# Chunk 1 transposed by TensorE instead of by DMA, rows of chunk 2 in one burst behind chunk 1's, casts of chunk 2's last batch sooner, rows of chunk 3 behind its transpose

## The chip, the cores and the metric

One core of one Trainium2 chip. The metric is the device time of one execution in microseconds. The granted clock is the share of full speed that the throttle allowed TensorE, 1.00 being all of it. Positions inside an execution are microseconds from the start of the profiled span, which is some 1.7 us shorter than the time.

## The reference

A retention recurrence (4 batches, 8 heads, 768 steps, head size 64), then a two-layer MLP with a tanh GELU (512 to 2048 to 512), all in float32:

```python
for t in range(S):
    state = gamma * state + einsum('bhd,bhe->bhde', k[:, :, t], v[:, :, t])
    y[:, :, t] = einsum('bhd,bhde->bhe', q[:, :, t], state) / sqrt(D)
x = y.transpose(0, 2, 1, 3).reshape(B * S, H * D)
h = x @ w_in
g = 0.5 * h * (1 + tanh(c * (h + 0.044715 * h**3)))
out = g @ w_out
```

## The kernel before

The sequence is cut into six chunks of 128 steps. For each chunk and each of four batches the kernel loads the rows of q, k and v (256 KB each, on SyncE's queue), casts q and k to 16 bits on ScalarE, transposes them, forms the scores A, masks them on VectorE, forms y, updates the state, and then runs the expert layers over all four batches. Chunk c's output matmuls and expert matmuls carry chunk c+1's attention between them: `run` issues the units of one in order, and `after` says what comes behind each unit (a unit is a small group of matmuls, mostly eight, and the copies that follow). In the traces each engine works its own list in order, and so does SyncE: a DMA transpose that waits for its cast holds back every load behind it. In the kernel before, SyncE issued nothing from 63.37 to 65.35, when chunk 2's first two casts had just ended (65.32), and the v rows behind that transpose went out from 66.63 on.

Chunk 0 is transposed by TensorE, all later chunks by DMA:

```python
def mm_T(c, b):                       # used by chunk 0
    ps = bank("att", F16, (128, 2, NHP, 128), "qkT_ps")
    for i, nm in enumerate("qk"):
        for hp in range(NHP):
            nc.tensor.transpose(out=ps[:, i, hp], in_=pair(h16[nm, c, b], hp), identity=iden)
    pss["T", c, b] = ps
def ev_T(c, b, eng=nc.vector):
    copy_on(eng, qkT_tile(c, b), pss.pop(("T", c, b)))
def dma_T(c, b):                      # chunks 1 to 5
    nc.sync.dma_start_transpose(out=qkT_tile(c, b)..., in_=qk16.pop((c, b))...)
def prep_qk(c, b):
    prep1(AC, "q", c, b)              # cast on ScalarE
    prep1(AC, "k", c, b)
    dma_T(c, b)
# ... output units of chunk 0, with chunk 1's attention behind them
    3: [(preps, 1, 0), (loads, 1, "v1", "q2", "k2")],
    5: [(preps, 1, 1), (load_dec,), (loads, 1, "q3", "k3", "v2")],
    8: [(att_1A, 0), (preps, 1, 2), (loads, 1, "v3")],
    10: [(att_1A, 1)],
# ... expert units of chunk 1
    10: [(prep_qk, 2, 2)],
    11: [(g_sums, PO, 1, 0, 4, 1, 2), (loads, 3, "q0", "k0", "q1", "k1")],
# ... output units of chunk 1
    0: [(prep_qk, 2, 3), (loads, 3, "v0", "v1", "q2", "k2", "q3", "k3", "v2", "v3")],
    4: [(att_AY, 2, (0, 1), "h", 2, (2, 3), AC)],
```

`s_p`, `s_u` and `s_q` are ScalarE's copies of partial products out of PSUM. `s_g` are sums of g, made by GpSimd for chunk 1, that the output matmuls read.

## Time and profile before

| | before |
|---|---|
| median | 217.24 us (3 runs, 217.07 to 219.27) |
| span of the profiled run | 216.2 us |
| TensorE busy | 198.3 us, 92% |
| SyncE's DMA queue, packet time as a share of 16 engines' span | 51.9% |
| TensorE waits for DMA transposes | 7.4 us in two waits |

### The profile page before, as it was taken

How to read it: one execution, taken by the hardware profiler on the slowest of the kernel's cores; microseconds unless marked ns; L12 is line 12 of the kernel's file. 1: busy time of each engine (PE TensorE's matmuls, PEld its weight loads, DVE VectorE, ACT ScalarE, POOL GpSimd, SP SyncE). 2: the span in 40 equal slices, each digit the busy share in tenths (PEclk: the TensorE clock that was granted, in tenths of full speed). 3: DMA queues.
4: the chain of work that ended last, by engine and by line, in shares of the span. 5: the costliest groups of instructions: out<-in, count | busy, mean ns of one | idle time of the engine just before them, and what ended most of it. 6: DMA issues, size and time to landing. Idle time of an engine off the chain costs nothing.

```text
span 216.2 us, 4616 instructions
## 1 busy us (share of the span) xinstructions
PE 198.3 (92%) x1916; PEld 135.0 (62%) x1916; DVE 89.2 (41%) x195; ACT 101.4 (47%) x180; POOL 111.5 (52%) x112
## 2 busy tenths in 40 slices
PE   5789999839999957999999999999999999999993
PEld 1447648626777845864478854488844688644882
DVE  3445489227750415730128710418600456134421
ACT  2384564432459601646662447563266412367321
POOL 0595000112378998145999528999339991200000
PEclk9999999997999996999999999999999999999999
DMA  7999999999998999999995699943440000310004
GB/s 162 288 251 207 206 207 218 238 196 243 299 253 184 176 227 232 229 225 249 233 232 100 27 271 273 235 104 69 97 194 3 2 3 2 133 64 0 0 15 182
DMA packets 102837, 35.28 MB, mean 163 GB/s; under 512 B 96544, under 2 KB 101024, under 8 KB 102816
## 3 DMA queue, kind: packets, MB, share of 16 engines
q1 hardware_dynamic: 90624, 23.45, 51.9%
q0 software_dynamic: 5664, 9.44, 17.9%
q10 hardware_dynamic: 6528, 2.10, 3.8%
q8 instruction: 15, 0.25, 0.5%
q14 instruction: 6, 0.05, 0.1%
HBM read 27.63 MB, written 6.29 MB: 157 GB/s over the span
## 4 chain that ended last, share of the span: by engine, by line
PE 69%; DMA 16%; ACT 5%; SPq 4%; POOL 3%; issue 1%; DVE 0%
PE h_ps L351 30%; PE o_ps L459 27%; DMA w_out<-in_moe_w_out_dram 7%; DMA k<-in_k_dram 5%; DMA qkT<-qk 4%; SPq L85 4%; PE y_ps L247 3%; PE a_ps L210 3%; PE y_ps L234 3%; PE o_ps L563 2%; ACT qk L145 2%; ACT g L367 2%; POOL qk L161 1%; PE s_ps L271 1%; POOL w_in L332 1%; POOL w_out L341 1%
## 5 line engine op out<-in xcount | busy, mean ns | idle before, releaser
L351 PE MATMUL h_ps<-xT,w_in 128*128 128x512 f16 (+2 forms) x488 | 87.5, 334 | 1.4 <-ACT g L367 1.1
L367 ACT ACTIVATE g<-h_ps 128x512 f16<-128x512 f32 (+1 forms) x98 | 57.2, 588 | 33.7 <-PE h_ps L351 33.7
L351 PEld LDWEIGHTS <-w_in 128*128 128x128 f16 x488 | 45.4, 98 | 38.7 <-issue 3.7
L223 DVE TENSOR_TENSOR a_sb<-a_ps,mask 128x512 f16<-128x512 f32 x48 | 30.1, 683 | 53.9 <-PE a_ps L210 53.9
L390 POOL TENSOR_TENSOR s_g<-g 128x512 f16<-128x512 f16 x32 | 36.9, 1153 | 13.2 <-ACT g L367 13.2
L459 PEld LDWEIGHTS <-s_g 128*128 128x128 f16 x320 | 30.5, 99 | 4.8 <-issue 0.2
L161 POOL TENSOR_TENSOR v<-v,cst 128x512 f16<-128x512 f32 x20 | 20.4, 1043 | 22.4 <-DMA v<-in_v_dram 17.7
L459 PE MATMUL o_ps<-t_w,s_g 128*128 128x256 f16 x240 | 28.5, 277 | 0.0
L459 PEld LDWEIGHTS <-g 128*128 128x128 f16 x240 | 23.5, 98 | 3.6
L390 POOL TENSOR_TENSOR s_g<-s_g,g 128x512 f16<-128x512 f16 x16 | 18.4, 1152 | 1.3
L390 POOL TENSOR_TENSOR s_g<-g,s_g 128x512 f16<-128x512 f16 x16 | 18.5, 1154 | 0.0
L459 PE MATMUL o_ps<-w_out,g 128*128 128x256 f16 x160 | 18.3, 273 | 0.0
L263 DVE TENSOR_TENSOR xT<-y_ps,dec 128x512 f16<-128x512 f32 x20 | 13.1, 687 | 11.9 <-PE y_ps L247 11.9
L210 PE MATMUL a_ps<-qkT 64*128 64x128 f16 x192 | 8.7, 225 | 7.7 <-DMA qkT<-qk 7.4
L492 POOL DMA_DIRECT2D out_dram<-o_sb x8 | 5.9, 737 | 18.0 <-DVE o_sb L390 14.4
L145 ACT CAST qk<-q 128x512 f16<-128x512 f32 x20 | 12.4, 618 | 5.4 <-DMA q<-in_q_dram 5.4
L482 ACT COPY s_u<-o_ps 128x512 f32<-128x512 f32 (+1 forms) x6 | 3.1, 516 | 22.8 <-PE o_ps L459 17.5
L145 ACT CAST qk<-k 128x512 f16<-128x512 f32 x20 | 12.4, 619 | 2.7 <-DMA k<-in_k_dram 2.7
L210 PEld LDWEIGHTS <-qkT 64*128 64x128 f16 x192 | 5.6, 97 | 12.2 <-DMA qkT<-qk 7.8
L488 ACT COPY o_sb<-o_ps 128x512 f32<-128x512 f32 (+1 forms) x5 | 2.7, 544 | 22.4 <-PE o_ps L459 22.4
L390 DVE TENSOR_TENSOR s_g<-g 128x512 f16<-128x512 f16 x16 | 6.7, 421 | 12.6 <-ACT g L367 12.6
L390 DVE TENSOR_TENSOR o_sb<-o_ps,s_p 128x512 f32<-128x512 f32 (+1 forms) x7 | 4.3, 615 | 17.5 <-ACT qk L145 8.0
(59 smaller groups left out, 167.9 us busy)
## 6 DMA issues: line engine op xcount, KB each, us to landing
k<-in_k_dram SPq DMA_DIRECT2D x22, 256.0 KB, 4.3
q<-in_q_dram SPq DMA_DIRECT2D x22, 256.0 KB, 4.3
v<-in_v_dram SPq DMA_DIRECT2D x22, 256.0 KB, 4.2
out_dram<-o_sb POOLq DMA_DIRECT2D x10, 512.0 KB, 3.7
w_in<-in_moe_w_in_dram POOLq DMA_DIRECT2D x4, 512.0 KB, 8.8
w_out<-in_moe_w_out_dram POOLq DMA_DIRECT2D x4, 512.0 KB, 14.1
q<-in_q_dram ACTq DMA_DIRECT2D x2, 256.0 KB, 3.9
v<-in_v_dram ACTq DMA_DIRECT2D x2, 256.0 KB, 5.3
```

The lines of the kernel that those rows point to most:

```text
L85: eng.dma_start(out=ld_tile(nm, c, b), in_=srcs[nm][b, :, c * C:(c + 1) * C, :].rearrange("h p d -> p h d"),)
L145: eng.copy(out=out, in_=in_)
L161: eng.tensor_tensor(out=t, in0=src, in1=cst[:, col:col + H].unsqueeze(2).broadcast_to([128, H, Dh]), op=ALU.mult,)
L210: nc.tensor.matmul(out=ps[j][:, hp], lhsT=t[j * 64:(j + 1) * 64, 1, hp], rhs=t[j * 64:(j + 1) * 64, 0, hp], start=True, stop=True,)
L223: nc.vector.tensor_tensor(out=s, in0=ps[j], in1=mask[:, j], op=ALU.mult)
L234: nc.tensor.matmul(out=y_ps[sl, hp], lhsT=st[sl, b, hp], rhs=qkT[c, b][sl, 0, hp], start=(hp == 0), stop=False, skip_group_check=True,)
L247: nc.tensor.matmul(out=y_ps[j * 64:(j + 1) * 64, hp], lhsT=h16["v", c, b][:, 2 * hp + j], rhs=a_sb[c, b, j][:, hp], start=(c == 0), stop=True,
L263: nc.vector.tensor_tensor(out=x, in0=ps, in1=dec, op=ALU.mult)
L351: nc.tensor.matmul(out=out, lhsT=w_in_sb[wi][:, kc, wr * 128:(wr + 1) * 128], rhs=xT[c][:, kc, t0:t1], start=(kc == 0), stop=(kc == NHP - ...
L367: nc.scalar.activation(out=out, in_=in_, func=AF.Gelu_apprx_tanh, scale=1.0)
L390: eng.tensor_tensor(out=out, in0=in0, in1=in1, op=op)
L459: nc.tensor.matmul(out=po, lhsT=lhs(c, lk, fp, a), rhs=rhs(rk, fp), start=(new and fp == 0 and (last or a == 0)), stop=(stop and fp == NP ...
```

## The change

Its intent is to take TensorE's two waits for DMA transposes away. (1) Chunk 1, whose rows and transposes all crowd into the queue at once, goes through TensorE. (2) The rows of chunk 2 are issued right behind chunk 1's. (3) Batch 3 of chunk 2 is cast four units sooner (behind expert unit 12 of 0 to 15, instead of behind the first output unit), and chunk 3's rows are queued behind its transpose instead of partly ahead.

```diff
     def prep_qk(c, b):
         prep1(AC, "q", c, b)
         prep1(AC, "k", c, b)
-        dma_T(c, b)
+        if c > 1:
+            dma_T(c, b)
+    def att_T(b, eng=VE):
+        mm_T(1, b)
+        ev_T(1, b, eng)
-    loads(1, "q0", "k0", "q1", "k1", "v0")
+    loads(1, "q0", "k0", "q1", "k1", "v0", "q2", "k2", "v1", "q3", "k3")
+    load_dec()
+    loads(1, "v2", "v3")
+    for nm in ("qk", "v"):
+        loads(2, *[x + str(b) for b in range(B) for x in nm])
 # output units of chunk 0
-            3: [(preps, 1, 0), (loads, 1, "v1", "q2", "k2")],
-            5: [(preps, 1, 1), (load_dec,), (loads, 1, "q3", "k3", "v2")],
-            8: [(att_1A, 0), (preps, 1, 2), (loads, 1, "v3")],
+            3: [(preps, 1, 0)],
+            5: [(att_T, 0), (preps, 1, 1)],
+            7: [(att_1A, 0)],
+            8: [(att_T, 1)],
+            9: [(preps, 1, 2)],
             10: [(att_1A, 1)],
-            11: [(mm_Y, 0, "h"), (ev_Y, 1, 0), (preps, 1, 3), (loads, 2, "q0", "k0", "q1", "k1")],
-            12: [(mm_Y, 1, "att"), (ev_Y, 1, 1), (mm_s, 1, (0,))],
+            11: [(mm_Y, 0, "h"), (att_T, 2, AC), (ev_Y, 1, 0)],
+            12: [(mm_Y, 1, "att"), (ev_Y, 1, 1), (mm_s, 1, (0,)), (preps, 1, 3)],
 # expert units of chunk 1 (the other loads of chunk 2 leave their places here too)
+            0: [(att_T, 3)],
-            11: [(g_sums, PO, 1, 0, 4, 1, 2), (loads, 3, "q0", "k0", "q1", "k1")],
+            11: [(g_sums, PO, 1, 0, 4, 1, 2)],
+            12: [(prep_qk, 2, 3), (load, 3)],
 # output units of chunk 1
-            0: [(prep_qk, 2, 3), (loads, 3, "v0", "v1", "q2", "k2", "q3", "k3", "v2", "v3")],
```

More of the change, by code (lines that the diff above doesn't have):

```diff
@@ L747 @@
     )
-    loads(2, "q2", "k2", "q3", "k3")
     run(
@@ L761 @@
             5: [(mm_Y, 3, "o"), (ev_Y, 1, 3)],
-            6: [(att_S, 1, 3), (prep_qk, 2, 0), (loads, 2, "v0", "v1")],
+            6: [(att_S, 1, 3), (prep_qk, 2, 0)],
             7: [(g_sums, PO, 1, 4, 8, 0, 1)],
-            8: [(prep_qk, 2, 1), (loads, 2, "v2", "v3")],
+            8: [(prep_qk, 2, 1)],
             10: [(prep_qk, 2, 2)],
-            11: [(g_sums, PO, 1, 0, 4, 1, 2), (loads, 3, "q0", "k0", "q1", "k1")],
+            11: [(g_sums, PO, 1, 0, 4, 1, 2)],
+            12: [(prep_qk, 2, 3), (load, 3)],
             14: [(att_AY, 1, (), "o", 2, (0, 1), None), (prep1, PO, "v", 2, 0), (prep1, PO, "v", 2, 1)],
```

## The prediction

> **What bounds the kernel now.** I read the page's slices first, then TensorE's waits from 30 us on, then TensorE's timeline around each wait, then windows over the same stretches, and last the queues that feed the waits. TensorE is busy for 92% of the span, so what can be gained is where it isn't. The page's two TensorE rows:
>
> ```profile
> PE   5789999839999957999999999999999999999993
> PEclk9999999997999996999999999999999999999999
> ```
>
> Each digit is 5.4 us. Apart from the start and the tail there are two holes, at slices 9 and 16, and the granted clock falls in the slice of each hole or the one after. The waits of TensorE from 30 to 100 us (total us, times, longest) name what made them:
>
> ```profile
> PE a_ps L210 <- DMA qkT<-qk: 7.4, 2, 3.9
> PE o_ps L563 <- ACT s_p L541: 0.9, 1, 0.9
> ```
>
> So two waits for DMA transposes of q and k cost 7.4 us, and one wait for a ScalarE copy 0.9. TensorE's timeline (start, duration, what, idle before) shows both waits and what follows them:
>
> ```profile
> 43.06 1.04 PE L563 MATMUL o_ps<-t_w,s_g 128*128 128x256 f16 x8
> 47.61 0.40 PE L210 MATMUL a_ps<-qkT 64*128 64x128 f16 x8 [3.52 <-DMA qkT<-qk]
> 47.94 1.74 PE L563 MATMUL o_ps<-t_w,s_g 128*128 128x256 f16 x8
> ...
> 82.54 0.61 PE L210 MATMUL a_ps<-qkT 64*128 64x128 f16 x8 [3.85 <-DMA qkT<-qk]
> 83.08 1.07 PE L247 MATMUL y_ps<-a_sb,v 128*64 128x128 f16 x16
> 84.08 3.56 PE L459 MATMUL o_ps<-t_w,s_g 128*128 128x256 f16 x24
> ```
>
> The same eight 256-wide matmuls take 1.04 us before the first wait and 1.74 after it: the wait is followed by a slow clock. Windows over the two stretches (PE busy, ..., POOL busy, then granted clock, DMA, GB/s):
>
> ```profile
> 47.60:51.60 4.00, 3.99 (x36) 2.40 (x36) 3.27 (x5) 1.41 (x3) 0.05 (x1) 0.57 1.25 261
> 82.50:87.60 5.10, 5.06 (x50) 3.86 (x52) 3.68 (x6) 1.62 (x3) 3.17 (x4) 0.69 1.09 246
> ```
>
> The clock was 0.57 for 4.0 us and 0.69 for 5.1 us: 4.0 x 0.43 = 1.72 us and 5.1 x 0.31 = 1.58 us lost on top of the waits. The queue that issues the transposes (SyncE's) shows why they are late:
>
> ```profile
> 41.97 2.27 SPq L200 DMA_TRANSPOSE qkT<-qk  x1
> ...
> 74.71 0.58 SPq L85 DMA_DIRECT2D q<-in_q_dram  x1
> 75.34 0.58 SPq L85 DMA_DIRECT2D k<-in_k_dram  x1
> 75.96 1.47 SPq L85 DMA_DIRECT2D q<-in_q_dram  x1
> 77.48 0.85 SPq L85 DMA_DIRECT2D k<-in_k_dram  x1
> 78.51 2.00 SPq L200 DMA_TRANSPOSE qkT<-qk  x1
> ```
>
> The first (chunk 1, batch 1) is issued at 41.97 and lands 5.6 us later. The second (chunk 2, batch 3) is issued only behind four row loads of chunk 3, though its casts had ended at 75.1.
>
> **What the Trainium skill says.** "TensorE: Matmul & The Clock Gate", Part 1: The HAM clock gate: about 3.4 us of idleness puts the array at half rate, and about 3.4 us of activity brings it back. The trace agrees: waits of 3.52 and 3.85 us are followed by clocks of 0.57 and 0.69, and a stretch with only the 0.86 us wait keeps 1.00. The same page, Part 4: PE-mode transpose: a transpose is a matmul against an identity, into PSUM, so a copy must follow; around 275 ns each in one kernel. Here:
>
> ```profile
> L190 PE MATMUL qkT_ps<-iden,qk x32: 219/248/314, 6.2 to 16.8; 128*128 128x128 f16 x32
> L145 ACT COPY qkT<-qkT_ps x3: 1006/1012/1013, 7.6 to 12.7; 128x1024 f16<-128x1024 f16 x3
> L147 DVE COPY qkT<-qkT_ps x1: 692/692/692, 17.1 to 17.1; 128x1024 f16<-128x1024 f16 x1
> ```
>
> That agrees for one, but they are pipelined: chunk 0's third set of eight starts at 12.08 and the next matmul at 12.53, so eight cost 0.45 us. "Advanced Engine Details and Errata", X-Bar Transpose (TRN2), has transpose DMAs as fast as regular ones. The trace differs: a 256 KB load follows the last by about 1 us (the casts that wait for q, k, q, k begin at 36.37, 37.22, 38.27, 39.29), while with a transpose in flight, between 44.6 and 46.6 us, the engines moved 39 GB/s against 256 from 36 to 38. I take a DMA transpose to hold up the queue by about 2 us.
>
> **The change part by part.** It has three parts.
>
> (1) Chunk 1's four DMA transposes become 32 TensorE transposes and four copies (three on VectorE, 0.69 us each; one on ScalarE, 1.01). The first wait goes: 3.52, with its slow clock 1.72, sum 5.24 us. TensorE gets 4 x 0.45 = 1.80 us. The first set falls before the wait for the s_p copy (0.86 us), which depends on ScalarE's cast of the second k, not on TensorE; it hides there: net -1.35 us. Walking the new order from 38.55 with the durations above: transpose 0 at 38.6 (its casts ended 37.8), s_p done as before at 40.4, scores 0 at 41.3 (copied by 39.8), transpose 1 at 42.5, its copy behind the scores' mask work (two of 0.68 us) until 43.9, scores 1 at 44.3, transpose 2 near 46.2, its ScalarE copy by 47.9, scores 2 near 48.9. None waits, with 0.3 us to spare at the tightest. Chunk 1's first expert matmul starts near 50.8 instead of 55.08. Transpose 3 takes a PSUM bank that the first state update must have left; VectorE does that behind two masks, so I put 0.4 us of wait there.
>
> (2) Chunk 2's 16 row loads are issued right behind chunk 1's. Chunk 1's 12 and the decay table land by about 36.4 + 12 x 1 = 48.4; chunk 2's q and k by 57 and its v by 61, or about 4 us later if chunk 0's two output stores (512 KB each) come between. ScalarE casts the first at about 60. The loads hence cause no wait, nor do they save one: in the kernel before ScalarE found chunk 2's rows there as well (no idle time ahead of its casts from 64.2 on).
>
> (3) Batch 3's casts go from the start of the output stage to expert unit 12, and chunk 3's loads behind its transpose. Cast at about 66, transposed and landed by about 72 with the worst landing time in the trace (5.6 us), needed near 76. The second wait goes: 3.85 + 1.58 = 5.43 us. ScalarE gets a pair of casts (1.02 us) in the stage where it and TensorE are about even (casts and two GELUs 2.1 us per two units, TensorE 1.97): up to 0.1 us.
>
> Sum: 5.24 + 5.43 - 1.35 - 0.4 - 0.1 = 8.8 us.
>
> **The rivals.**
>
> A, GpSimd takes over as the bound behind the second wait. Its sums of g for chunk 1 run without a gap from 65.90:
>
> ```profile
> 77.04 1.15 POOL L390 TENSOR_TENSOR s_g<-g 128x512 f16<-128x512 f16 x1
> 78.27 1.15 POOL L390 TENSOR_TENSOR s_g<-s_g,g 128x512 f16<-128x512 f16 x1
> ```
>
> The second of these ends at 79.42 and the output unit after the wait reads it. TensorE would reach that unit at 84.08 less 3.85 and less about 0.7 of slow clock, 79.5: slack of 0.1 us where there were 4.7. Both move forward together with the expert stage, so I expect a wait between nothing and 0.5 us. Were GpSimd also held up by the v rows, it could eat 1 to 2 us: about 210.
>
> B, the loads in one burst slow what is needed first. Chunk 1's batches 2 and 3 and the decay table now queue only behind each other, and lose three transposes of 2 us ahead of them, so they land sooner than before; but if SyncE's issue stalls (it took up to 3.3 us a load between 59 and 63), the rows of batch 2 (estimate 42.4, needed 44.0) delay ScalarE, and with it s_q and the copies. Gain cut to about 6 us: 211.
>
> C, the copies. 2.07 us more on VectorE and 1.01 on ScalarE inside a chain of TensorE, copy, mask, TensorE. If the slack of 0.3 us is wrong, each set waits up to 0.7 us: 2 us less gain, 210.5.
>
> D, the waits were hidden anyway: against it speaks that the chain of waits runs through both transposes (4.4% of the span, 9.5 us of 216.2).
>
> **Range and chances.** 217.24 - 8.8 = 208.4; I put 208.5, with GpSimd's wait taking a little. If A, B or C comes true in part, 210 to 211.5; if the bank wait and the copies cost nothing and the steady part keeps every microsecond, 207. For less than 2% (above 212.9) half of the gain must be lost, for which I see no single mechanism: 7%. Slower would need a new long wait: 1%.
>
> **What would show it.** Right: no TensorE wait on a DMA transpose between 38 and 90 us; granted clock 1.00 in both stretches; the first chunk-1 expert matmul near 50.8, the output stage near 70 instead of 73.27, the 64-matmul expert stage of chunk 2 (97.05) near 88.3, and everything behind shifted by the same. Each step wrong: a wait of a_ps on VectorE's or ScalarE's qkT copy (C), of ScalarE's casts on row loads between 44 and 66 us (B), of the output stage on s_g from GpSimd at its second product (A), a wait of the fourth transpose well above 0.4 us (the bank). A clock below 1.00 without an idle stretch would break the estimate of the slow clock.

## More of the kernel before

The lines that carry the argument are shown in the prediction. Two more of the page, to be compared later: the queue of SyncE (packets, MB, share) and the chain of work that ended last, by engine.

```profile
q1 hardware_dynamic: 90624, 23.45, 51.9%
...
PE 69%; DMA 16%; ACT 5%; SPq 4%; POOL 3%; issue 1%; DVE 0%
```

A bound engine would hold the whole chain. Here DMA holds 16% of it: part of that is the start, part are the two waits.

## The result, and the profile after

| | before | changed |
|---|---|---|
| median | 218.25 us (4 runs, 217.07 to 219.73) | 209.64 us (4 runs, 208.82 to 209.74) |
| ratio | | 0.9594 (95% interval 0.9516 to 0.9672) |
| span of the profiled run | 216.2 us | 207.1 us |

Ratios are the mean time of one kernel's fast runs over that of the other's of the same rounds, so not quite the ratio of the medians quoted. The four runs of the kernel before are the three above and one more. Faster by 4.1%. A second series of the changed kernel (below) gave 0.9598.

The changed kernel's page: TensorE's busy share and its granted clock over the span, the DMA queue of SyncE, and the chain by engine.

```profile
PE   5789999899999999999999999999999999999993
...
PEclk9999999999999999999999999999999999999999
...
q1 hardware_dynamic: 86400, 22.40, 50.0%
...
PE 75%; DMA 12%; ACT 5%; POOL 4%; SPq 3%; issue 0%; DVE 0%
```

Both holes are gone, and with them both dips of the clock. TensorE has 75% of the chain instead of 69, DMA 12 instead of 16. The queue moved 1.05 MB less, which are four transposes of 256 KB. Its packet time fell from 0.519 x 216.2 = 112.2 us to 0.500 x 207.1 = 103.6: 2.1 us for each transpose, where row loads landed about 1 us apart (the prediction's four casts). Packet time itself scatters: another execution of the changed kernel had 0.493 x 207.0 = 102.1.

TensorE's waits from 30 to 100 us in the changed kernel (total us, times, longest):

```profile
PE o_ps L563 <- ACT s_p L541: 1.0, 1, 1.0
PE h_ps L351 <- ACT g L367: 0.7, 2, 0.5
```

No wait for a DMA transpose is left. The same stretches as before on TensorE's timeline:

```profile
42.99 0.61 PE L190 MATMUL qkT_ps<-iden,qk 128*128 128x128 f16 x8
43.44 0.60 PE L530 MATMUL o_ps<-t_w,s_g 128*128 128x256 f16 x4
...
44.84 0.40 PE L210 MATMUL a_ps<-qkT 64*128 64x128 f16 x8
45.17 1.05 PE L563 MATMUL o_ps<-t_w,s_g 128*128 128x256 f16 x8
...
51.17 1.05 PE L351 MATMUL h_ps<-xT,w_in 128*128 128x256 f16 x8
52.05 0.61 PE L190 MATMUL qkT_ps<-iden,qk 128*128 128x128 f16 x8
...
75.45 0.64 PE L247 MATMUL y_ps<-a_sb,v 128*64 128x128 f16 x16
76.02 2.79 PE L459 MATMUL o_ps<-t_w,s_g 128*128 128x256 f16 x24
```

Transpose 1 starts at 42.99 and the next matmul at 43.44: 0.45 us. Scores 1 begin at 44.84 without a wait, and the eight wide matmuls behind them take 1.05 us where they took 1.74. The 24 matmuls of the output stage take 2.79 us instead of 3.56. GpSimd's second sum, which those 24 read, is this one:

```profile
74.87 1.15 POOL L390 TENSOR_TENSOR s_g<-s_g,g 128x512 f16<-128x512 f16 x1
```

It ends at 74.87 + 1.15 = 76.02, the very moment at which TensorE begins: the trace shows no slack there, and no wait either.

Where the time came from, by positions in the two traces (us):

| | before | changed | gained so far |
|---|---|---|---|
| first expert matmul of chunk 1 | 55.01 | 51.17 | 3.8 |
| output stage of chunk 1 begins | 73.27 | 69.87 | 3.4 |
| output unit behind the second wait | 84.08 | 76.02 | 8.1 |
| expert stage of chunk 2, behind its wait for a GELU | 97.05 | 88.22 | 8.8 |
| end of the span | 216.2 | 207.1 | 9.1 |

So 3.8 us come at the first wait, 0.4 are given back (the fourth transpose), and 5.4 come at the second, about 0.8 of them in the slow stretch behind 84.08; from there on the difference hardly changes, and the last 0.3 us are not explained.

### The profile page after: what moved, and what is told of

Its sections match the earlier page's. It is cut to its first block, busy times and chain, and to the rows that moved or that the text cites. A ratio compares the mean times of both kernels' runs of the same rounds, so it can differ in the third digit from the quotient of the medians.

```text
span 207.1 us, 4685 instructions
## 1 busy us (share of the span) xinstructions
PE 196.6 (95%) x1948; PEld 135.2 (65%) x1948; DVE 91.0 (44%) x198; ACT 102.1 (49%) x181; POOL 111.5 (54%) x112
## 4 chain that ended last, share of the span: by engine, by line
PE 75%; DMA 12%; ACT 5%; POOL 4%; SPq 3%; issue 0%; DVE 0%
PE h_ps L351 31%; PE o_ps L459 30%; DMA w_out<-in_moe_w_out_dram 7%; DMA k<-in_k_dram 5%; PE y_ps L247 3%; PE y_ps L234 3%; PE o_ps L563 3%; PE a_ps L210 3%; ACT qk L145 2%; SPq L85 2%; ACT g L367 2%; POOL qk L161 2%; PE s_ps L271 1%; POOL w_in L332 1%; POOL w_out L341 1%; PE qkT_ps L190 1%
## 5 line engine op out<-in xcount | busy, mean ns | idle before, releaser
L390 POOL TENSOR_TENSOR s_g<-g 128x512 f16<-128x512 f16 x32 | 36.9, 1152 | 11.8 <-ACT g L367 11.8
L459 PE MATMUL o_ps<-t_w,s_g 128*128 128x256 f16 x240 | 27.8, 273 | 0.0
L288 DVE SCALAR_TENSOR_TENSOR st<-st,cst,s_ps 128x128 f16<-128x128 f16 (+1 forms) x40 | 10.0, 315 | 0.5 <-PE s_ps L271 0.5
L459 PE MATMUL o_ps<-w_out,s_g 128*128 128x256 f16 x80 | 9.6, 273 | 0.0
```

Source lines behind the costliest of these rows:

```text
L288: nc.vector.scalar_tensor_tensor(out=t[:, :, hp], in0=t[:, :, hp], scalar=cst[:, OG + hp:OG + hp + 1], in1=s_ps[:, :, hp], op0=ALU.mult, o ...
L390: eng.tensor_tensor(out=out, in0=in0, in1=in1, op=op)
L459: nc.tensor.matmul(out=po, lhsT=lhs(c, lk, fp, a), rhs=rhs(rk, fp), start=(new and fp == 0 and (last or a == 0)), stop=(stop and fp == NP ...
```

## The experiments

Twelve runs, in three series. The first two were on one chip, the third on another; the kernel before was run in each series, with medians of 219.04, 217.10 and 218.33 us. The changed kernel was run again in the third alone. Small differences are therefore read from the ratios or within a series. How much the rows' landing scatters shows in the copy s_p, up to which the kernel before, the run of part 3 alone and the two runs with filled waits have identical instructions: the matmul behind it began at 40.4, 41.3, 40.7 and 40.8.

**Part 1 alone.** Chunk 1 by TensorE; loads, casts of chunk 2 and everything else where they were.

```diff
+            if c > 1: dma_T(c, b)          # and att_T as in the change
-            8: [(att_1A, 0), (preps, 1, 2), (loads, 1, "v3")],
+            7: [(att_1A, 0)],
+            8: [(att_T, 1), (loads, 1, "v3")],
+            9: [(preps, 1, 2)],            # ... the rest of att_T as in the change
```

> Part 1 alone: chunk 1 by TensorE, the row loads and batch 3's casts of chunk 2 where they were. By my sum (5.24 - 1.35, and no bank wait, since the changed kernel showed none) it gains 3.9 us: some 1.8% under the kernel before; the first wait is gone with its slow clock, the second stays at about 3.9 us with a slow clock behind it. If chunk 1's wait was hidden by something else (rival), the gain is under 1 us.

Measured: 215.74 us, ratio 0.987 (0.982 to 0.992), 3.3 us by the medians of the series. Its timeline shows both halves of the answer:

```profile
45.56 0.40 PE L210 MATMUL a_ps<-qkT 64*128 64x128 f16 x8
...
70.43 0.40 PE L210 MATMUL a_ps<-qkT 64*128 64x128 f16 x8 [0.88 <-DMA qkT<-qk]
...
81.75 0.61 PE L210 MATMUL a_ps<-qkT 64*128 64x128 f16 x8 [4.68 <-DMA qkT<-qk]
```

The first wait is gone and the time fell by more than the noise, so the wait was not hidden by anything. But TensorE now comes sooner to chunk 2's transposes than they land: a new wait of 0.88 us, and the second wait is 4.68 instead of 3.85. A part of the gain is taken back by the queue. How much can't be read from this trace: it is the slowest of the six executions (217.53 us), with a granted clock of 0.83 over its first 20 us, where the kernel before had 1.00.

**Part 3 alone.** The sooner cast and chunk 3's loads behind the last transpose of chunk 2.

```diff
-            11: [(g_sums, PO, 1, 0, 4, 1, 2), (loads, 3, "q0", "k0", "q1", "k1")],
+            11: [(g_sums, PO, 1, 0, 4, 1, 2)],
+            12: [(prep_qk, 2, 3), (load, 3)],
-            0: [(prep_qk, 2, 3), (loads, 3, "v0", ...)],
```

> Part 3 alone: batch 3 of chunk 2 cast at expert unit 12, chunk 3's loads behind its transpose; chunk 1 by DMA transposes as before. By my sum 5.4 us gained, about 2.5%: the second wait gone, the first still 3.5 us. If the loads' burst were what made the second wait go (rival), the wait stays and the gain is under 1 us.

Measured: 215.44 us, ratio 0.985 (0.979 to 0.991), 3.6 us. The second wait is gone: 24 matmuls start at 81.29 and take 2.79 us. So the burst is not what removes it. But the gain is smaller than 5.4, and a reason stands in TensorE's and ScalarE's timelines:

```profile
94.97 5.34 PE L351 MATMUL h_ps<-xT,w_in 128*128 128x512 f16 x24 [1.96 <-ACT g L367]
```

```profile
89.07 0.62 ACT L145 CAST qk<-q 128x512 f16<-128x512 f32 x1 [1.81 <-DMA q<-in_q_dram]
...
92.95 0.62 ACT L145 CAST qk<-q 128x512 f16<-128x512 f32 x1 [1.04 <-DMA q<-in_q_dram]
93.80 0.62 ACT L145 CAST qk<-k 128x512 f16<-128x512 f32 x1 [0.24 <-DMA k<-in_k_dram]
94.33 1.08 ACT L367 ACTIVATE g<-h_ps 128x512 f16<-128x512 f32 x2
```

Chunk 3's rows start to be issued at 78.05 (69.45 in the changed kernel, 74.71 before), so ScalarE waits for them and the first GELUs of chunk 2 come late: 1.96 us of wait instead of 0.48. In this execution the copy s_p was late as well (1.86 us of wait instead of 0.86), which is scatter. The two parts alone give 3.3 and 3.6 us, 6.9 together, and the whole change 8.6: each gains more with the other there. The traces put this down to the queue, since what either part takes from TensorE's waits brings TensorE or ScalarE sooner to transfers that have not landed.

**The change without the burst.**

```diff
-    for nm in ("qk", "v"):
-        loads(2, *[x + str(b) for b in range(B) for x in nm])
+    # chunk 2's loads at their four old places
```

> The changed kernel with chunk 2's 16 row loads back at their four old places. My theory: they save nothing by coming early, so the same time as the changed kernel within 0.5 us (some 4% under the kernel before), and the copy s_p perhaps 0.3 to 0.6 us sooner, because the rows of batch 1 share the queue with fewer others. Rival: the early rows are what lets the casts and the v rows be on time; then ScalarE or GpSimd waits for rows of chunk 2, and 1 to 4 us are lost.

Measured: 210.23 us, ratio 0.960 (0.955 to 0.965): the changed kernel's within the interval. Two of six executions are left out as slow: one of 213.12 us, 1.5% above the fastest, and the profiled one, which took 334.75 us at a mean granted clock of 0.571 (1.00 in the first 10 us, 0.56 from there to the end).

> The kernel without the burst once more, for a profile of a fast run (the last one fell in a run with a granted clock of 0.571). My theory, that the burst is not needed once parts 1 and 3 are done: no TensorE wait on a DMA transpose, ScalarE's casts of chunk 2 without a wait for rows from 60 us on, and the copy s_p waited for by 0.5 to 1.0 us. Rival: small waits for rows or transposes of chunk 2 that just balance a sooner s_p.

Measured: 210.43 us in one run. TensorE waited 0.3 us for one transpose of chunk 2, 1.5 us for s_p, and 1.3 us for the first GELU of chunk 2 (0.5 in the changed kernel). ScalarE's casts of chunk 2 waited for no rows, as expected; the wait for a transpose and the longer one for s_p were not. No worth of the burst can be told from none once parts 1 and 3 are done: the ratio leaves room for about 1 us either way, and the small waits are as large as the scatter of the rows' landing.

**The burst alone**, on the kernel before, with DMA transposes for chunk 1.

```diff
+    loads(1, ..., "v2", "v3"); loads(2, all)   # ahead of everything, as in the change
     3: [(preps, 1, 0)], ...                    # DMA transposes as before
```

> The kernel before with part 2 alone: all rows of chunks 1 and 2 in a burst, chunk 1 still by DMA transposes, which the one queue then issues behind 29 loads, near 62 us. The first scores of chunk 1 wait until about 66 instead of 42, so 18 to 24 us more than before, less up to 5 us if the second wait goes: 230 to 240 us. Rival: the engines serve the queue out of order enough for the transposes to pass; then within 5 us of before.

Measured: 231.06 us, ratio 1.058 (1.054 to 1.063). TensorE's first scores of chunk 1:

```profile
62.89 0.61 PE L210 MATMUL a_ps<-qkT 64*128 64x128 f16 x8 [20.18 <-DMA qkT<-qk]
```

SyncE issued the first transpose at 58.73, behind the rows, and TensorE stood for 20.18 us. The cost, 12.7 us, is at the low end of what was expected: 20.18 less the 3.52 of the old first wait, less the 5.43 of the second wait and its clock, which did not come back, plus 0.5 for the only other wait for a transpose, makes 11.8. This is what part 1 makes possible: with chunk 1's transposes off the queue nothing urgent stands behind the burst.

**The waits filled with dummy matmuls**, on the kernel before, to tell idleness and slow clock apart.

```diff
-            10: [(att_1A, 1)],
+            10: [(warm, 14), (att_1A, 1)],      # 14 matmuls of 512 columns on zeros
-            4: [(att_AY, 2, (0, 1), "h", 2, (2, 3), AC)],
+            4: [(warm, 16), (att_AY, 2, (0, 1), "h", 2, (2, 3), AC)],
```

> The kernel before, whose two waits are filled with 14 and 16 dummy matmuls of 512 columns (0.216 us each, 3.0 and 3.5 us), and nothing else. If the idleness makes the slow clock, the two transposes land as late as before, but the clock stays at 1.00 behind them: about 3.0 us less, 1.4%. If the slow clock has another cause, the same time as before or a few tenths more.

Measured: 218.75 us, ratio 0.997 (0.991 to 1.003): no gain that can be told from none. The timeline:

```profile
44.18 3.19 PE L728 MATMUL warm_ps<-zero 128*128 128x512 f16 x14
47.89 0.40 PE L210 MATMUL a_ps<-qkT 64*128 64x128 f16 x8 [0.53 <-DMA qkT<-qk]
48.22 1.05 PE L563 MATMUL o_ps<-t_w,s_g 128*128 128x256 f16 x8
...
73.30 0.61 PE L210 MATMUL a_ps<-qkT 64*128 64x128 f16 x8 [2.31 <-DMA qkT<-qk]
73.83 1.89 PE L351 MATMUL h_ps<-xT,w_in 128*128 128x256 f16 x8
```

The first wait ends where it did before (47.89 against 47.61), but the matmuls behind it take 1.05 us, not 1.74, and the expert stage begins 1.2 us sooner (53.77). From the end of the wait to the expert stage it is 5.9 us instead of 7.4, so the slow clock was worth 1.5 us here (1.72 by the prediction's estimate). So idleness does make the slow clock. What was gained was lost at the next transpose of chunk 2, which landed no sooner (2.31 us of wait, and a slow clock behind that). The second filling was too long: the transpose had landed at 78.56 + 4.1 = 82.7, while the scores that need it came only near 84.8.

Filling the second wait alone, with 14, was to mend that:

> The kernel before with 14 dummy matmuls (3.0 us) in its second wait alone, behind which no further DMA transpose of chunk 2 is waited for. If idleness makes the slow clock and this costs the path 1.58 us there: the wait's end stays where it was, the clock behind it is 1.00, and the time falls by about 1.5 us (0.7%). Rival: what is gained there is lost to the next wait, as with the first wait in the run that filled both; then within 0.3 us of before.

Measured: 218.09 us, ratio 1.006 (0.999 to 1.013). The clock behind it was full (24 matmuls in 2.79 us), but here too TensorE came late, after a wait of 1.70 us for an earlier transpose, so that the filling outlasted the landing (82.9) by about 1.3 us. That the slow clock follows the idleness is shown in both runs; what it is worth in the end, in the time of the whole kernel, is not shown by either.

**What made the second wait: the late cast or the loads ahead of the transpose?** The changed kernel, with the cast late again but chunk 3's loads still behind it.

```diff
-            12: [(prep_qk, 2, 3), (load, 3)],
+            0: [(prep_qk, 2, 3), (load, 3)],      # output stage of chunk 1, as before
```

> The changed kernel, with batch 3 of chunk 2 cast late again (behind the first unit of the output stage, about 71), but chunk 3's loads still behind its transpose. If the four loads ahead of it in the queue made the second wait: the transpose is issued near 72 and lands at 75 to 76, needed at 75.2, so a wait of 0 to 1 us, and 0 to 2.5 us more than the changed kernel because chunk 3's rows come later. If the late cast made it: a wait near 3.9 us with a slow clock, and 5 us more.

Measured: 210.47 us, ratio 0.970 (0.963 to 0.977), against 0.959 (0.952 to 0.967) for the changed kernel: perhaps 1% more, but the intervals overlap. TensorE's scores of batches 2 and 3, and its first wait in chunk 2's expert stage:

```profile
76.37 0.62 PE L210 MATMUL a_ps<-qkT 64*128 64x128 f16 x16
...
90.89 9.29 PE L351 MATMUL h_ps<-xT,w_in 128*128 128x512 f16 x42 [1.68 <-ACT g L367]
```

The transpose was issued at 73.2, landed 2.7 us later, and nobody waited for it. So the four loads ahead of it made the wait. What this costs is the other side: chunk 3's rows are issued from 74.48 on, and TensorE waits 1.68 us for the first GELU. Waits of 0.5 and 0.6 us for chunk 2's first two transposes came on top, at the same place where the changed kernel had none. The profiled execution is the slowest of the five (211.80 us), so it shows more than the median lost.

The same was not tried for chunk 1, and it is an open rival to part 1: its casts of batch 1 ended at 39.91 in the kernel before, but SyncE issued three rows (39.39 to 41.87) ahead of the transpose at 41.97. Whether the first wait would go, at no cost to TensorE, with these rows behind the transpose is not shown.

**Two ScalarE waits removed**, the 1.03 us for s_p and the 0.48 for the first GELU of chunk 2.

```diff
-            5: [(att_T, 0), (preps, 1, 1)],
+            5: [(att_T, 0)],
+            6: [(preps, 1, 1)],
-            13: [(prep_qk, 3, 3)],
+            12: [(prep_qk, 3, 3)],
```

> The changed kernel with two pairs of casts moved on ScalarE: batch 1 of chunk 1 behind the copy s_p, batch 3 of chunk 3 ahead of the last copy of the output stage. TensorE's waits of 1.03 us (s_p) and 0.48 us (first GELU of chunk 2) should fall to about 0.2 and 0: 1.0 to 1.4 us less than the changed kernel, about 4.6% under the kernel before. Rival: the first scores and transposes then wait for the later cast, or for rows, and nothing is gained.

Measured: 208.88 us, ratio 0.963 (0.958 to 0.967), not to be told from the changed kernel. A miss, and the waits of TensorE (over the whole execution) say why:

```profile
PE a_ps L210 <- DMA qkT<-qk: 1.1, 2, 0.6
...
PE o_ps L563 <- ACT s_p L541: 0.2, 1, 0.2
```

Both waits shrank as meant, to 0.2 us and nothing (the matmuls behind chunk 2's first GELU start without one). TensorE then came to chunk 2's first two transposes sooner than they landed: 1.1 us. In the changed kernel the second of them is issued at 64.5, takes 4.0, and is needed at 68.7: 0.2 us of slack.

**The v rows moved behind the transposes**, on top of the last.

```diff
-    for nm in ("qk", "v"):
-        loads(2, *[x + str(b) for b in range(B) for x in nm])
+    loads(2, *[x + str(b) for b in range(B) for x in "qk"])
-            8: [(prep_qk, 2, 1)],
-            10: [(prep_qk, 2, 2)],
+            8: [(prep_qk, 2, 1), (loads, 2, "v0", "v1")],
+            10: [(prep_qk, 2, 2), (loads, 2, "v2", "v3")],
```

> The changed kernel with the two moves of casts, and chunk 2's v rows no longer in the burst but behind its second and third transposes. In the run with the moved casts alone both gains were taken back by waits of 0.52 and 0.58 us for chunk 2's first two transposes, the first issued behind four v rows, landing after 5.1 us. My theory: with nothing ahead of them they land in about 3 us, those waits go, and the time is 1.0 to 1.5 us less than the changed kernel. Rival: the v rows then come too late for GpSimd, whose sums stand right at TensorE's need; the same time as the changed kernel or more.

It was run in one series with the changed kernel itself:

> The changed kernel itself once more, on the same chip and in the same rounds as the next three, to compare them with: 0.955 to 0.965 of the kernel before.

Measured: the changed kernel 209.53 us, ratio 0.960 (0.956 to 0.963); this one 210.75, ratio 0.965 (0.960 to 0.970). No wait for a transpose was left, as expected, and still it is slower:

```profile
90.19 9.72 PE L351 MATMUL h_ps<-xT,w_in 128*128 128x512 f16 x44 [2.35 <-ACT g L367]
```

With v rows between the transposes the last transpose is issued at 70.99 and chunk 3's first row at 73.13; ScalarE waits for those rows, and TensorE waits 2.35 us for the GELU. Another 0.8 us went at 50.8 to the decay table, which landed late in this execution; nothing ahead of it in the queue was changed, so this is scatter. Neither my theory nor the rival named the right victim: it was chunk 3's q and k on ScalarE, not chunk 2's v on GpSimd.

**Chunk 2 on TensorE as well.**

```diff
-        if c > 1:
+        if c > 2:
             dma_T(c, b)            # and att_T for chunk 2 behind expert units 8, 10, 12, 13
```

> The changed kernel with chunk 2's four transposes on TensorE as well. Each set costs TensorE 0.45 us in a stage where it and ScalarE are the bound and no DMA transpose is waited for: 1.8 us more than the changed kernel. Rival: chunk 2's DMA transposes hold the queue so long that chunk 3's rows come sooner without them; then less than 1 us more.

Measured: 210.64 us, ratio 0.964 (0.961 to 0.967), 1.1 us more than the changed kernel of the same series, between the two expectations (the intervals of the two ratios overlap). The expert stage of chunk 1 took 19.9 us (51.51 to 71.45) against 18.7 (51.07 to 69.77): of the 1.8 us that the four sets take on TensorE, 1.2 show. No version beat the changed kernel by more than the noise.

## Why the prediction was right

The time lies in the range: 209.64 against 208.5 predicted. With one more run (219.73) the median of the kernel before is 218.25, 1.0 above the number that the prediction started from; from there its 8.8 us give 209.4. The measured difference is 8.6 by medians and 9.1 between the profiled spans.

- **First wait and its clock, 5.24 less 1.35.** Right in place and nearly in size: the first expert matmul at 51.17 was predicted near 50.8, a gain of 3.8 us there instead of 4.3 (from 55.01; the prediction's 55.08 is 0.07 off). The set of eight costs 0.45 us each time, as measured in chunk 0. The first set did hide behind s_p: TensorE still waited 1.0 us for that copy. The copy itself came 0.37 us later than before, because the second k's cast began at 39.66 instead of 39.29; that is inside the scatter between identical kernels. The rest of the 0.5 is about the size by which the slow clock was put too high, 1.72 instead of the 1.5 of the run with filled waits.
- **Fourth transpose, 0.4 us of bank wait.** Mis-sized: none. It began at 52.05, straight behind the eight matmuls ahead of it, so only its own 0.45 us was paid. This and the next term are luck for the sum: the gain before the second wait is 3.4 us as computed (5.24 - 1.35 - 0.4 - 0.1) because 0.5 us too much at the first wait and 0.5 us of costs that did not come cancel out.
- **Second wait and its clock, 5.43.** Right: the gain grew from 3.4 to 8.1 us at this place and to 8.8 behind the stretch that had been slow, 5.4 in all. The reason given, four loads ahead of the transpose, is shown by the run with the late cast.
- **ScalarE's extra pair of casts, 0.1.** Nothing to be seen: the expert stage has the same single 0.19 us wait in both traces.
- **Part 2 saves and costs nothing.** Right within the noise for the whole change (0.960 without it). The prediction did not say that alone it costs 12.7 us.
- **Rival A, GpSimd at the second product.** Stood at the edge as computed, the sum ending at 76.02 and TensorE starting at 76.02, and cost nothing that the trace records as a wait. B and C did not come: chunk 2's casts waited for no rows, and no score matmul waited for a copy of transposes.
- **The sum.** It was right for the change as a whole, but its terms are not worth singly what they say. Alone, part 1 gave 3.3 us of the 3.9 expected and part 3 gave 3.6 of 5.4. What the prediction missed is the coupling through the one queue: transposes and rows land at the queue's pace, and what TensorE gains at one wait it can lose at the next landing.

## What to carry to other kernels

When a wait for a DMA is removed, ask what stands next in the same queue: here part 1 alone and the two moved casts gave back part of their gain to the next landing, and four early loads ahead of one transpose had made a wait of 3.85 us. Transfers that someone waits for go ahead of those that only have to come in time, but whatever is pushed back has a reader too; moving v rows or casts by a few positions just moved the wait. A transpose moved to the bound engine cost 0.45 us a set and paid where TensorE waited for the DMA's transposes (chunk 1); where it did not (chunk 2), the time was 1.1 us longer for four.

## What the Trainium skill lacked or had wrong

- "Advanced Engine Details and Errata", X-Bar Transpose (TRN2), has transpose DMAs as fast as regular ones. Taking chunk 1's four out cut the queue's packet time by 8.6 us between the two profiled runs, 2.1 us each for 256 KB, against about 1 us between the landings of row loads of that size; from issue to landing they took 2.7 us in a quiet queue and up to 6.5 us behind rows. Over the other traces packet time was 109.5 to 111.9 us with chunk 1's four and 100.8 to 105.8 without (the execution at the low clock left out), again about 2 us each. Taking chunk 2's four out as well saved 0.493 x 207.0 less 0.476 x 208.9 = 2.6 us in one pair of traces; with a scatter this large it is not shown that they cost less.
- "TensorE: Matmul & The Clock Gate", Part 1: The HAM clock gate, gives about 3.4 us of idleness for the fall to half rate. Once 2.31 us was enough (a clock of 0.58 over the next 4.0 us), while waits of 1.70, 1.96 and 2.35 us left it at 1.00. The page calls the window free-running; no run here shows where it lay.
- The same page, Part 4: PE-mode transpose, gives around 275 ns for one. It has no figure for several in a row: eight took 0.45 us at full clock, 56 ns each.
- The same page, Part 1, tells of a clock seen stuck low for over 50 us. Here one execution of a kernel that otherwise takes 210 us ran at 0.56 from its first 10 us to its end and took 334.75 us; why is not shown.
